# A fused attention and two MoE layers: a new order of the work, another load of the normalisation's gains, and a split last store

## The chip, the cores and the metric

The kernel runs on one core of a Trainium2 chip. The metric is the device time of one execution in microseconds, the median of three runs. A profile of one further execution goes with it; its times are those of that execution.

## The reference

The input has 4 batches of 576 tokens and 8 heads of 64. Three layers follow each other.

```
scores = q k^T / 8;  masked to 0 <= i - j < 64;  softmax;  x = attn v          # [2304, 512]
h  = x w_in;  s = h * softmax(h);  ln = (s - mean) / sqrt(var + 1e-6) * g_ln    # d_ff 1024
x2 = ln w_out                                                                   # [2304, 512]
h  = x2 w2_in;  g = (a0 + a1 h + a2 h^2 + a3 h^3) / (1 + |b0||h| + |b1| h^2 + 1e-6)   # d_ff 2048
out = g w2_out                                                                  # [2304, 512] float32
```

The MoE weights arrive as 64-bit floats.

## The kernel before

**Tiles and stages.** The 2304 tokens are 18 tiles of 128. Attention and the first MoE layer work tile by tile: `scores` (matmuls in PSUM, with the band mask added by matmuls with `ib` and `masks` for tiles 0 to 7, and by VectorE from `limits` for tiles 8 to 17), `max`, eight `exp` on ScalarE, `sum` and `rcp`, two `norm` on GpSimd, `probs` (transposes on TensorE), `probs_copy`, `attend`, `att_hi` and `att_lo` (x as a sum of two parts), `h0` to `h3` (one step for each 128 rows of w_in), then the softmax and normalisation of h, its transposes `lnT`, and for three tiles together `x2`. x2 goes to DRAM. The second MoE layer works on blocks of 4, 4, 4, 3 and 3 tiles: pairs of `g` steps, an elementwise chain on ScalarE and VectorE, and `o` steps. Each product is made of three matmuls with split operands, but for `h` of tiles 0 and 1, which use plain float32.

**Weights.** 64-bit words are turned into float32 by a chain of ScalarE and VectorE steps (`cv0` to `cv7`). The units are `i` (w_in: two halves of a half megabyte for rows 0 to 127, then three of one megabyte), `o` (w_out, four of one megabyte) and `c` (both weights of the second layer, sixteen of one megabyte). The `c` units are spilled to DRAM as float32 (`w2d`) and read back later. Two loaded units (`x64`) and two converted ones (`cA`) fit at a time.

**gT.** `g_ln` is loaded as [128, 8], column c holding elements 128c to 128c + 127, and multiplied by -0.5 on GpSimd (lines 842 and 843). The conversion of w_out's parts multiplies by it.

**The order.** Nothing is issued in the order of the code. Each piece of work is a *step* with an engine, a duration, needs and buffers; `Schedule` (line 29) works out an order in Python while the kernel is built. `latest` gives each step a due time, worked back from wanted times and from what needs it; the table `SHIFT`, one number for each group of steps, moves these due times. `arrange` then simulates: among the steps that can start at the earliest moment it picks the one with the earliest due time. A DMA's result counts as landed 2.0 us after the DMA's own duration (line 158), the DMA queue is one resource that starts at 0.9 us (`AT`), and `PORT` names VectorE steps that may not run beside GpSimd's. `RINGS` holds the number of buffers; q and k have two each, the scores one. `gaps` puts filler matmuls ahead of TensorE's early steps where the plan has idle time. The order that comes out is issued as it is: every engine, and the SP queue with all DMAs, runs its own list in order and waits where something is not ready. So the durations in the code are the planner's costs, not measured times, and they only decide the order.

**The end.** The last block's last tile is finished last: `o_last`, then `o_copy` (512 columns on ScalarE or VectorE) and `o_store` (256 KB from SP).

Of the kernel before, what the change touches and what calls it, by code (L numbers as in the profile page):

```python
# [28 lines left out]
class Schedule:  # L29
# [14 lines left out]
    PORT = ("cv1", "cv2", "cv3", "cv6", "cv7", "ln_apply", "w2")  # L44
    AT = {"DMA": 0.9, "POOL": 0.7, "DVE": 0.8, "ACT": 0.8}
# [54 lines left out]
    def arrange(self):  # L100
# [38 lines left out]
        while ready:  # L139
# [18 lines left out]
            done[key] = t + dur + (2.0 if e == "DMA" else 0.0), e  # L158
# [16 lines left out]
    def gaps(self):  # L175

        idle, end = {}, 0.0
        for t, _, key, e in self.order:
            if e == "PE":
                if key[0] == "h0":  # L180
                    break
                idle[key] = max(0, int((t - end - 0.3) / 0.25)) if end else 0
                end = t + self.steps[key][1][0]
        return idle
# [69 lines left out]
    "solu_max.s": -23.79, "solu_exp.s": -2.77, "solu_mul.s": 187.84, "ln_square.s": 171.01, "ln_eps.s": 70.47,  # L254
    "ln_var.s": -132.84, "ln_root.s": -12.34, "ln_newton.s": -33.03, "ln_apply.s": 195.97, "lnT0.s2": -32.79,
# [51 lines left out]


PLAIN = 8


NORMP = 0

# [6 lines left out]
def attention_moe_moe2(ctx: ExitStack, tc, q, k, v, w1, w1o, g_ln, w2, w2o, num, den, out):  # L320
# [5 lines left out]
    nc = tc.nc  # L326
# [850 lines left out]
```

## Time and profile before

| | us |
|---|---|
| median of three runs (710.07 to 711.42) | 710.61 |
| the profiled execution | 714.31 |
| its span, first to last instruction | 712.5 |
| TensorE busy | 686.9 (96%) |
| VectorE busy | 579.7 (81%) |
| ScalarE busy | 484.4 (68%) |
| GpSimd busy | 62.3 (9%) |

The profile's span covers the instructions; the execution's own time is 1.8 us longer. PE is TensorE, DVE is VectorE, ACT is ScalarE, POOL is GpSimd, SP is the engine that issues the DMAs; PEld is the loading of weights into TensorE. Busy shares are means over stages with different limits. Lines are those of the kernel before.

### The profile page before, as it was taken

How to read it: one execution, taken by the hardware profiler on the slowest of the kernel's cores; microseconds unless marked ns; L12 is line 12 of the kernel's file. 1: busy time of each engine (PE TensorE's matmuls, PEld its weight loads, DVE VectorE, ACT ScalarE, POOL GpSimd, SP SyncE). 2: the span in 40 equal slices, each digit the busy share in tenths (PEclk: the TensorE clock that was granted, in tenths of full speed). 3: DMA queues.
4: the chain of work that ended last, by engine and by line, in shares of the span. 5: the costliest groups of instructions: out<-in, count | busy, mean ns of one | idle time of the engine just before them, and what ended most of it. 6: DMA issues, size and time to landing. Idle time of an engine off the chain costs nothing.

```text
span 712.5 us, 11368 instructions
## 1 busy us (share of the span) xinstructions
PE 686.9 (96%) x4356; PEld 591.6 (83%) x4356; DVE 579.7 (81%) x863; ACT 484.4 (68%) x878; POOL 62.3 (9%) x96
## 2 busy tenths in 40 slices
PE   5799999999899999999999999999999999999997
PEld 5557789789788989998888888888888889999896
DVE  5799998889798854687999787888778877878773
ACT  5799976676676844667876566675755756566662
POOL 3333202112220120000000000000000000000000
PEclk9999999999999999999999999999999999999999
DMA  8966437775968414604331030000300001000101
GB/s 267 333 199 202 167 140 254 247 246 184 333 197 293 153 46 126 199 1 163 103 99 51 0 104 0 1 1 0 104 1 0 1 1 59 1 1 7 38 1 45
DMA packets 44982, 77.81 MB, mean 109 GB/s; under 512 B 4672, under 2 KB 23104, under 8 KB 44544
## 3 DMA queue, kind: packets, MB, share of 16 engines
q1 hardware_dynamic: 44928, 77.09, 32.6%
q8 instruction: 34, 0.56, 0.3%
q14 instruction: 20, 0.16, 0.1%
HBM read 59.25 MB, written 17.83 MB: 108 GB/s over the span
## 4 chain that ended last, share of the span: by engine, by line
PE 70%; DVE 12%; DMA 7%; ACT 7%; issue 2%; SPq 1%; ACTq 0%; DVEq 0%
PE hp L964 9%; PE hp L963 9%; PE hp L962 9%; PE o L1029 9%; PE o L1030 9%; PE o L1028 9%; DMA w2d<-cc 5%; PE x L747 3%; PE x L749 3%; PE x L748 3%; DMA xi<-in_moe_w_in_dram 1%; ACT P L501 1%; PE h L671 1%; PE h L670 1%; PE h L669 1%
## 5 line engine op out<-in xcount | busy, mean ns | idle before, releaser
L962 PE MATMUL hp<-x2h,w 128*128 128x512 f32 (+1 forms) x320 | 118.1, 369 | 0.0
L964 PE MATMUL hp<-x2h,w 128*128 128x512 f32 (+1 forms) x320 | 117.9, 368 | 0.0
L963 PE MATMUL hp<-x2l,w 128*128 128x512 f32 (+1 forms) x320 | 117.7, 368 | 0.0
L1030 PE MATMUL o<-w,gl 128*128 128x512 f32 x288 | 112.6, 391 | 0.0
L1029 PE MATMUL o<-w,gh 128*128 128x512 f32 x288 | 112.5, 391 | 0.0
L1028 PE MATMUL o<-w,gh 128*128 128x512 f32 x288 | 112.0, 389 | 0.0
L982 DVE SCALAR_TENSOR_TENSOR w<-r,b,w 128x1024 f32<-128x1024 f32 (+1 forms) x40 | 47.0, 1176 | 53.1 <-ACT r L976 53.1
L974 ACT ACTIVATE w<-hp,ab 128x1024 f32<-128x1024 f32 (+1 forms) x40 | 41.3, 1032 | 67.9 <-PE hp L964 47.7
L1013 ACT CAST gh<-t 128x1024 fp32r<-128x1024 f32 (+1 forms) x40 | 38.6, 965 | 58.1 <-PE o L1029 43.8
L747 PE MATMUL x<-lh,wo 128*128 128x384 f32 x192 | 66.0, 344 | 1.4 <-ACT xs L361 1.4
L962 PEld LDWEIGHTS hp<-x2h,w 128*128 128x128 f32 x320 | 60.1, 188 | 8.7
L963 PEld LDWEIGHTS hp<-x2l,w 128*128 128x128 f32 x320 | 60.1, 188 | 8.6
L964 PEld LDWEIGHTS hp<-x2h,w 128*128 128x128 f32 x320 | 60.1, 188 | 7.5
L749 PE MATMUL x<-lh,wo 128*128 128x384 f32 x192 | 64.3, 335 | 0.0
L748 PE MATMUL x<-ll,wo 128*128 128x384 f32 x192 | 64.3, 335 | 0.0
L1030 PEld LDWEIGHTS o<-w,gl 128*128 128x128 f32 x288 | 54.0, 188 | 11.2
L1029 PEld LDWEIGHTS o<-w,gh 128*128 128x128 f32 x288 | 54.1, 188 | 10.7
L1028 PEld LDWEIGHTS o<-w,gh 128*128 128x128 f32 x288 | 54.1, 188 | 10.5
L521 POOL TENSOR_TENSOR P<-P,rc 128x512 f32<-128x512 f32 x36 | 45.5, 1280 | 111.9 <-DVE rc L513 76.3
L669 PE MATMUL h<-wi,xh 128*128 128x512 f32 x128 | 50.7, 396 | 1.8 <-DVE st L686 1.7
L357 DVE TENSOR_TENSOR gl<-t,gh 128x1024 fp32r<-128x1024 f32 (+1 forms) x40 | 44.5, 1112 | 8.9 <-ACT gh L1013 8.9
L671 PE MATMUL h<-wi,xl 128*128 128x512 f32 x128 | 50.4, 394 | 0.3 <-DVE xl L357 0.2
(113 smaller groups left out, 1442.6 us busy)
## 6 DMA issues: line engine op xcount, KB each, us to landing
v<-in_v_dram SPq DMA_DIRECT2D x35, 256.0 KB, 4.6
xc<-in_moe_w_in_dram SPq DMA_DIRECT2D x16, 512.0 KB, 4.0
xc<-in_moe_w_out_dram SPq DMA_DIRECT2D x16, 512.0 KB, 5.7
w2d<-cc SPq DMA_DIRECT2D x16, 512.0 KB, 6.5
r<-w2d SPq DMA_DIRECT2D x32, 256.0 KB, 2.9
k<-in_k_dram SPq DMA_DIRECT2D x17, 384.0 KB, 4.9
q<-in_q_dram SPq DMA_DIRECT2D x18, 256.0 KB, 5.3
x2d<-xs SPq DMA_DIRECT2D x6, 768.0 KB, 6.4
```

Of the source, the lines that this page charges most:

```text
L669: nc.tensor.matmul(o, xh[:, c, :], wh, start=(c == 0), stop=False)
L671: nc.tensor.matmul(o, xl[:, c, :], wh, start=False, stop=(c == KC - 1))
L747: nc.tensor.matmul(o, wh, lh[:, f, :], start=(f == 0), stop=False)
L748: nc.tensor.matmul(o, wh, ll[:, f, :], start=False, stop=False)
L749: nc.tensor.matmul(o, wl, lh[:, f, :], start=False, stop=(f == FC1 - 1))
L962: nc.tensor.matmul(h, wh[:, sl], xh[:, c], start=(c == 0), stop=False)
L963: nc.tensor.matmul(h, wh[:, sl], xl[:, c], start=False, stop=False)
L964: nc.tensor.matmul(h, wl[:, sl], xh[:, c], start=False, stop=(c == KC - 1))
L982: nc.vector.scalar_tensor_tensor(out=w, in0=r, scalar=b1, in1=w, op0=ALU.mult, op1=ALU.add)
L1028: nc.tensor.matmul(o, gh[:, n, sl], wh, start=(f == 0), stop=False)
L1029: nc.tensor.matmul(o, gh[:, n, sl], wl, start=False, stop=False)
L1030: nc.tensor.matmul(o, gl[:, n, sl], wh, start=False, stop=(f == FC2 - 1))
```

## The change

The steps' work is nearly the same. What changes:

- All of `SHIFT` is new, and some of the planner's costs are, so that the order of every engine is another one.
- A DMA counts as landed after 2.3 us instead of 2.0 us, and the DMA queue starts at 1.5 us.
- `g_ln` is loaded as 8 rows of 128 elements into a cleared [128, 128] tile, transposed on TensorE into PSUM, and multiplied by -0.5 on VectorE from there. `h0` of tile 0 comes after it, since both use the same PSUM tile.
- `ident`, `gR` and `ib` are made first on GpSimd, then the masks; the limits are a step of their own behind.
- Five filler matmuls precede TensorE's first step.
- The last tile's copy is made in two halves of 256 columns on ScalarE and VectorE, each with a store of its own, one issued from ScalarE and one from SP.
- A branch that was never taken (`NORMP = 0`) is removed.

```diff
-    PORT = ("cv1", "cv2", "cv3", "cv6", "cv7", "ln_apply", "w2")
-    AT = {"DMA": 0.9, "POOL": 0.7, "DVE": 0.8, "ACT": 0.8}
+    PORT = ("cv1", "cv2", "cv3", "cv6", "cv7", "ln_apply", "w2", "max_scale", "sum")
+    AT = {"DMA": 1.5, "POOL": 0.7, "DVE": 0.8, "ACT": 0.8}
...
-            done[key] = t + dur + (2.0 if e == "DMA" else 0.0), e
+            done[key] = t + dur + (2.3 if e == "DMA" else 0.0), e
...
-                idle[key] = max(0, int((t - end - 0.3) / 0.25)) if end else 0
+                idle[key] = max(0, int((t - end - 0.3) / 0.25)) if end else 5
...
 SHIFT = {
-    "cv.i_0_0": -234.63, "cv.i_0_512": 71.67, "cv.i_2_0": 195.23, "cv.i_3_0": 193, "cv.o_0": 120.63,
-    "load_q.1": -26.18, "load_k.1": 5.41, "load_v0.0": 95.7, "load_v1.0": 1.71, "load_q.2": 0.09, "load_k.3": -3.15,
...
+    "cv.i_0_0": -434.33, "cv.i_0_512": 87.02, "cv.i_1_0": 1.81, "cv.i_2_0": 203.88, "cv.i_3_0": 204.67, "cv.o_0": 122.97,
+    "load_k.1": -0.8, "load_v0.0": 17.18, "load_v1.0": 16.34, "load_q.2": 68.07, "load_q.3": -11.97, "load_k.3": 42.51,
...
     def constants():
+        make_identity(nc, ident)
+        nc.gpsimd.memset(gR, 0.0)
+        nc.gpsimd.tensor_copy(ib, ident)
         nc.gpsimd.memset(band, 0.0)
...
+    def make_limits():
...
-        make_identity(nc, ident)
-        nc.gpsimd.tensor_copy(ib, ident)
...
+    def gT_rows():
+        nc.tensor.transpose(h_tile(0)[:, 0:P], gR, ident)
+
+    def gT_scale():
+        nc.vector.tensor_scalar_mul(gT, tiles["h", 0][:, 0:FC1], -0.5)
...
+            needs += [("gT", 0)] if (t, c) == (0, 0) else []
...
-    add(("constants", 0), "POOL", 4.5, None, [], constants)
-    add(("gT_load", 0), "DMA", 0.1, -60.0, [], lambda: nc.sync.dma_start(gT, g_ln.rearrange("(c p) -> p c", p=P)))
-    add(("gT", 0), "POOL", 0.3, None, [("gT_load", 0)], lambda: nc.gpsimd.tensor_scalar_mul(gT, gT, -0.5))
+    add(("constants", 0), "POOL", 3.9, None, [], constants)
+    add(("limits", 0), "POOL", 2.2, None, [("constants", 0)], make_limits)
+    add(("gT_load", 0), "DMA", 0.1, -60.0, [("constants", 0)], lambda: nc.sync.dma_start(gR[0:FC1], g_ln.rearrange("(c p) -> c p", p=P)))
+    add(("gT_rows", 0), "PE", 0.2, None, [("gT_load", 0)], gT_rows)
+    add(("gT", 0), "DVE", 0.12, None, [("gT_rows", 0)], gT_scale)
...
-            add(("cvl", *key), "DMA", 2.7, None, [], cv_load, key, *load, take=[("x64", key)], group=group)
+            add(("cvl", *key), "DMA", 2.55 if key[0] == "o" else 3.3, None, [], cv_load, key, *load, take=[("x64", key)], group=group)
...
-            add(("cv7", *key), "DMA", 1.46, want, [("cv6", *key)], cv_spill, key, give=[("cA", key)], group=group)
+            add(("cv7", *key), "DMA", 1.8, want, [("cv6", *key)], cv_spill, key, give=[("cA", key)], group=group)
...
-        add(("cvl", *key), "DMA", 1.42 if key[1] == 0 else 2.7, None, [], w1_load, key[1], cols,
+        add(("cvl", *key), "DMA", 1.35 if key[1] == 0 else 2.55, None, [], w1_load, key[1], cols,
...
+    def o_half(bk, j, n):
...
+        o = tiles["o", bk][j][:, n * DM // 2:(n + 1) * DM // 2]
+        copy((nc.scalar, nc.vector)[n], tiles["os", bk, j][n], o)
+
+    def o_store_half(bk, j, n):
+        r0 = (FIRSTS[bk] + j) * P
+        (nc.scalar, nc.sync)[n].dma_start(out[r0:r0 + P, n * DM // 2:(n + 1) * DM // 2], tiles["os", bk, j][n])
```

`SHIFT` has some 530 entries before and after; the lines of it shown here are put together from entries that concern the first loads.

## Rows read from the trace of the kernel before

**Rows 1.** The page's head.
```profile
span 712.5 us, 11368 instructions
```
**Rows 2.** Busy time by stage: PE, PEld, DVE, ACT, POOL; clock; DMA share; GB/s.
```profile
0.00:30.00 30.00, 19.28 (x220) 16.68 (x221) 19.10 (x29) 18.34 (x48) 11.39 (x28) 0.94 0.84 297
30.00:100.00 70.00, 65.08 (x673) 49.44 (x673) 68.53 (x131) 68.41 (x197) 17.72 (x25) 1.00 0.59 199
100.00:250.00 150.00, 143.76 (x1207) 128.59 (x1206) 131.81 (x319) 106.69 (x269) 27.65 (x34) 1.00 0.69 230
250.00:709.00 459.00, 458.75 (x2261) 396.90 (x2259) 360.29 (x387) 290.63 (x367) 5.51 (x10) 1.00 0.14 44
709.00:712.50 3.50, 0.00 (x0) 0.00 (x0) 0.00 (x0) 0.37 (x1) 0.00 (x0) 0.75 0.36 137
```
**Rows 3.** Timeline, 15 to 32 us: start, duration, work, idle time before and its releaser.
```profile
16.08 0.20 DVE L513 RECIPROCAL rc<-rc 128x8 f32<-128x8 f32 x1
...
17.84 0.26 POOL L843 TENSOR_SCALAR gT<-gT 128x8 f32<-128x8 f32 x1 [10.86 <-DMA gT<-in_moe_g_ln_dram]
18.07 3.09 POOL L521 TENSOR_TENSOR P<-P,rc 128x512 f32<-128x512 f32 x2
...
21.94 1.12 ACT L599 ACTIVATE xi<-xi 128x1024 f32<-128x1024 f32 x1 [4.03 <-DMA xi<-in_moe_w_in_dram]
...
23.09 0.69 DVE L604 TENSOR_SCALAR xi<-xi 128x1024 f32<-128x1024 f32 x1 [1.65 <-ACT xi L599]
...
24.00 0.59 ACT L361 COPY PT<-pt 128x512 f32<-128x512 f32 x1
...
26.38 0.17 DVE L509 TENSOR_SCALAR rc<-sum 128x8 f32<-128x8 f32 x1 [1.39 <-ACT P L504]
...
28.44 3.70 PE L663 MATMUL h<-xi,xh 128*128 128x512 f32 x8 [0.76 <-ACT xh L361]
```
**Rows 4.** Timeline of the SP queue, same columns.
```profile
3.13 7.12 SPq L450 DMA_DIRECT2D k<-in_k_dram  x2
...
12.06 0.58 SPq L581 DMA_DIRECT2D xi<-in_moe_w_in_dram  x1
...
14.69 2.89 SPq L443 DMA_DIRECT2D q<-in_q_dram  x2
```
**Rows 5.** DMA issues of the whole span: KB each, median us to landing.
```profile
w2d<-cc SPq DMA_DIRECT2D x16, 512.0 KB, 6.5
...
xi<-in_moe_w_in_dram SPq DMA_DIRECT2D x3, 1024.0 KB, 9.9
...
gT<-in_moe_g_ln_dram SPq DMA_DIRECT2D x1, 4.0 KB, 6.3
```
**Rows 6.** Two slices of the stage table; the last two columns are the DMA's.
```profile
14.00:15.00 1.00, 1.00 (x11) 1.00 (x10) 0.86 (x2) 1.00 (x5) 0.00 (x0) 1.00 0.63 137
...
16.00:17.00 1.00, 1.00 (x36) 0.94 (x35) 0.68 (x3) 1.00 (x2) 0.00 (x0) 1.00 1.00 410
```
**Rows 7.** Waits of ACT and PE, 100 to 250 us: total, times, longest.
```profile
ACT cc L599 <- DMA w2d<-cc: 19.7, 9, 5.3
...
PE pv L547 <- ACT PT L361: 3.7, 3, 1.6
```
**Rows 8.** Groups by shape (busy us, mean ns), and landings of the output's 18 stores.
```profile
L361 ACT COPY xs<-x 128x384 f32<-128x384 f32 x22 | 10.4, 473 | 13.4 <-PE x L749 10.8 <-DMA x2d<-xs 2.5
L361 ACT COPY os<-o 128x512 f32<-128x512 f32 x18 | 9.4, 592 | 6.0 <-PE o L1030 6.0
...
L363 DVE COPY xs<-x 128x384 f32<-128x384 f32 x2 | 1.1, 551 | 0.0
...
DMA to landing us min/median/max: 2.0/2.4/4.4
```
**Rows 9.** Timeline of PE: scores of tile 0 and of tile 1.
```profile
7.84 1.99 PE L478 MATMUL s<-k,q 64*64 64x128 f32 x32 [0.15 <-DMA q<-in_q_dram]
...
16.14 1.04 PE L478 MATMUL s<-k,q 64*64 64x128 f32 x32
```

More of the change, by code (lines that the diff above doesn't have):

```diff
@@ L208 @@
 SHIFT = {
[45 rows of a table removed]
-    "solu_max.s": -23.79, "solu_exp.s": -2.77, "solu_mul.s": 187.84, "ln_square.s": 171.01, "ln_eps.s": 70.47,
-    "ln_var.s": -132.84, "ln_root.s": -12.34, "ln_newton.s": -33.03, "ln_apply.s": 195.97, "lnT0.s2": -32.79,
[30 rows of a table removed]
-    "cv.c_15": -82.41, "load_coefficients.s": -15.43, "coefficients.s": 8.16, "close_attention.s": 11.01,
[16 rows of a table removed]
-    "g_hi.s": -21.03, "g_lo.s": 33.55, "o.s": -2.06,
[41 rows of a table added]
+    "h2.s2": -16.25, "h3.s2": 6.13, "solu_max.s": -11.77, "solu_mul.s": 3.5, "ln_square.s": 13.76, "ln_eps.s": -5.59,
+    "ln_var.s": -0.88, "ln_root.s": -1.46, "ln_apply.s": 71.68, "lnT0.s2": 57.07, "ln_hi0.s": 1.13,
[46 rows of a table added]
+    "g_n1.s": 32.93, "g_n2.s": 31.85, "g_hi.s": -12.04, "g_lo.s": 5.83, "o.s": 45.65,
 }
@@ L309 @@
 PLAIN = 8
-NORMP = 0
 RINGS = {"q": 2, "k": 2, "v": 4, "s": 1, "P": 2, "tr": 2, "PT": 4, "o": 2, "x": 2, "h": 1, "e": 2, "lnT": 2, "xs": 1,
@@ L384, in attention_moe_moe2 @@
     ident = cst.tile([P, P], F32, name="ident")
+    gR = cst.tile([P, P], F32, name="gR")
     ib = ap.tile([P, P], BF16, name="ib", tag="ib", bufs=1)
@@ L387, in attention_moe_moe2 @@
     limits = ap.tile([P, 3, P], F32, name="limits", tag="limits", bufs=1)
+    band = ap.tile([P, WIN], F32, name="band", tag="band", bufs=1)
     def constants():
-        band = ap.tile([P, WIN], F32, name="band", tag="band", bufs=1)
+        make_identity(nc, ident)
+        nc.gpsimd.memset(gR, 0.0)
+        nc.gpsimd.tensor_copy(ib, ident)
         nc.gpsimd.memset(band, 0.0)
@@ L503, in soft_exp @@
             return
-        nc.scalar.activation((tiles["s", t] if t < NORMP else Pn[t])[:, j, n, :], tiles["s", t][:, j, n, :], AF.Exp,
-                             bias=mx[:, c:c + 1], scale=0.125, accum_out=su[:, c:c + 1])
+        nc.scalar.activation(Pn[t][:, j, n, :], tiles["s", t][:, j, n, :], AF.Exp, bias=mx[:, c:c + 1], scale=0.125,
+                             accum_out=su[:, c:c + 1])
     def soft_sum(t):
@@ L513, in soft_rcp @@
         nc.vector.reciprocal(rc, rc)
-    def soft_norm_all(t):
-        nc.vector.tensor_tensor(out=Pn[t].rearrange("p j c k -> p (j c) k"), in0=tiles["s", t].rearrange("p j c k -> p (j c) k"),
-                                in1=stat[t][2].unsqueeze(2).broadcast_to([P, H, P]), op=ALU.mult)
     def soft_norm(t, j):
@@ L789, in attention_moe_moe2 @@
                 if t >= PLAIN:
-                    step(f"max{j}{n}", "DVE", 0.24, ["scores", ("constants", 0)], soft_max_of, t, j, n, give=[("s", t)])
-                step(f"exp{j}{n}", "ACT", 0.342, ["max_scale" if t < PLAIN else f"max{j}{n}"], soft_exp, t, j, n,
-                     give=[("s", t)] if NORMP <= t < PLAIN else [])
+                    step(f"max{j}{n}", "DVE", 0.215, ["scores", ("limits", 0)], soft_max_of, t, j, n, give=[("s", t)])
+                step(f"exp{j}{n}", "ACT", 0.342 if t < PLAIN else 0.392, ["max_scale" if t < PLAIN else f"max{j}{n}"], soft_exp, t, j, n,
+                     give=[("s", t)] if t < PLAIN else [])
         step("sum", "DVE", 0.12, [f"exp{j}{n}" for j in range(2) for n in range(4)], soft_sum, t)
         step("rcp", "DVE", 0.12, ["sum"], soft_rcp, t)
-        if t < NORMP:
-            step("norm", "DVE", 1.14, ["rcp"], soft_norm_all, t, give=[("s", t)])
-        for j in range(2) if t >= NORMP else ():
+        for j in range(2):
             step(f"norm{j}", "POOL", 1.08, ["rcp"], soft_norm, t, j)
         for j in range(2):
-            step(f"probs{j}", "PE", 0.44, [f"norm{j}" if t >= NORMP else "norm"], probs_T, t, j, want=WANT[f"probs{j}"], take=[("tr", (t, j))],
+            step(f"probs{j}", "PE", 0.44, [f"norm{j}"], probs_T, t, j, want=WANT[f"probs{j}"], take=[("tr", (t, j))],
                  give=[("P", t)])
@@ L838, in attention_moe_moe2 @@
                      take=[] if dc else [("xs", pr)], give=[("o", (t, 2 + dc))])
-            step("x2_store", "DMA", 1.5, ["x2_out3"], x2_store, pr, give=[("xs", pr)])
-    add(("constants", 0), "POOL", 4.5, None, [], constants)
-    add(("gT_load", 0), "DMA", 0.1, -60.0, [], lambda: nc.sync.dma_start(gT, g_ln.rearrange("(c p) -> p c", p=P)))
-    add(("gT", 0), "POOL", 0.3, None, [("gT_load", 0)], lambda: nc.gpsimd.tensor_scalar_mul(gT, gT, -0.5))
+            step("x2_store", "DMA", 2.2, ["x2_out3"], x2_store, pr, give=[("xs", pr)])
+    add(("constants", 0), "POOL", 3.9, None, [], constants)
[3 more added lines that the diff above has]
+    add(("gT", 0), "DVE", 0.12, None, [("gT_rows", 0)], gT_scale)
     def convert(key, want, *load):
@@ L1044, in o_store @@
         nc.sync.dma_start(out[r0:r0 + P, :], tiles["os", bk, j])
+    def o_half(bk, j, n):
+        if n == 0:
+            tiles["os", bk, j] = [pools["tp"].tile([P, DM // 2], F32, name=f"os{bk}_{j}_{m}", tag="xr", bufs=RINGS["xr"])
+                                  for m in range(2)]
+        o = tiles["o", bk][j][:, n * DM // 2:(n + 1) * DM // 2]
[3 more added lines that the diff above has]
+        (nc.scalar, nc.sync)[n].dma_start(out[r0:r0 + P, n * DM // 2:(n + 1) * DM // 2], tiles["os", bk, j][n])
     G = {3: 2.09, 4: 2.73}
@@ L1128, in attention_moe_moe2 @@
             for j in range(SIZES[bk]):
+                if (bk, j) == (NB2 - 1, SIZES[bk] - 1):
+                    for n, (e, d) in enumerate((("ACT", 0.3), ("DVE", 0.33))):
+                        add((f"oc{n}", bk, j), e, d, s3 + 2.0 + 0.1 * j, [("ol", j)], o_half, bk, j, n,
+                            take=() if n else [("xr", ("o", bk, j))])
+                        add((f"os{n}", bk, j), ("ACT", "DMA")[n], 0.4, s3 + 2.6 + 0.1 * j, [(f"oc{n}", bk, j)], o_store_half, bk, j, n)
+                    continue
                 add(("oc", bk, j), "ACT|DVE", (0.475, 0.6), s3 + 2.0 + 0.1 * j, [("ol", j) if bk == NB2 - 1 else ("o", i)], o_copy, bk, j,
```

178 rows, old and new, of the table SHIFT are left out of this document.

## The prediction

> **What bounds the kernel now.** I read the page first: the span is 712.5 us [rows 1]. Then the table by stages [rows 2]: from 250 us to 709 TensorE is busy in 458.75 of 459 us, so whatever is gained or lost before 250 us reaches the end one for one, and nothing behind 250 us but the tail can be gained by an order. TensorE's idle time sits in the first 30 us (10.7 us, and part of what is counted busy there is filler matmuls without use), in 30 to 100 us (4.9), in 100 to 250 us (6.2) and in the tail (3.5). The same table names the limits: in 30 to 100 us VectorE is busy in 68.53 of 70 us and ScalarE in 68.41, so that stage lasts as long as their work does, and it ends earlier only if that work starts earlier. In 100 to 250 us VectorE is at 88%, ScalarE at 71%: waits decide there, not the sum of work.
>
> Last the timeline of the start [rows 3]. The first h matmul of tile 0 begins at 28.44. Behind it lie two waits in program order. GpSimd's normalisation of tile 0 had its reciprocal at 16.28 (16.08 + 0.20) but began at 18.07, because the scaling of gT stood ahead of it in GpSimd's queue and waited for its DMA until 17.84. ScalarE sat idle for 4.03 us until 21.94, waiting for the third megabyte of w_in; the exponentials of tile 1 and the copy of tile 0's transposed probabilities (24.00) stood behind that instruction. VectorE lost 1.65 and 1.39 us in its wake.
>
> **The start: gT as rows, constants first.** *Removed from GpSimd:* one instruction of 0.26 us and its wait; the normalisation of tile 0 can begin 18.07 - 16.28 = 1.8 us sooner. Next late is then ScalarE's wait for w_in, which ends at 21.94 in either case, so alone this gains little at 28.44.
>
> *The load.* The column load of gT is 1,024 elements for 4 KB, with 6.3 us to landing [rows 5]. While it is in flight, the DMA engines move 137 GB/s at a share of 0.63 in one microsecond, against 410 at 1.00 in a later one [rows 6]: 0.63 x 410 - 137 = 121 KB, 0.3 us of full rate lost in that slice. As eight rows that goes; I count it as part of the gain on w_in's landing.
>
> *Added:* clearing gR on GpSimd (the clearing of ident's like size is some 0.2 us, an estimate by the 0.26 of gT's own instruction, rows 3), one transpose on TensorE and one small VectorE multiply. VectorE is full in the stage that follows, so the multiply counts: between 0 and the 0.26 us of the same operation on GpSimd; I take +0.2. The transpose costs nothing while TensorE waits anyway between scores 0, which ends at 9.83, and scores 1, which begins at 16.14 [rows 9]. It waits for a load that SP can issue once gR is clear, about where it issued its sixth load (3.13, rows 4); with the same 6.3 us it lands near 10. In TensorE's queue scores 1 and the probabilities of tile 0 stand behind it. The cover is some 6 us, and each microsecond beyond that is one microsecond later.
>
> *Constants.* The identity and the masks come first, the limits in a step behind. The first real scores matmul, at 7.84, waits for no constant but for q and k, so the time there is 0; the limits are read only from tile 8 on. The bound on the loss side is 0 too, since the same instructions run in the same queue, all done before the normalisation at 16 us. Five fillers now precede TensorE's first step. Scores 0 took 1.99 us where scores 1 took 1.04 [rows 9]; whether fillers that end some microseconds earlier change that, no row shows: between 0 and -0.95, and I take 0, as the matmuls right ahead of scores 0 did not help it either.
>
> The Trainium skill (TensorE: Matmul & The Clock Gate, "What's actually happening") has the array throttled by default and released by activity. Rows 9 agree in the durations, a factor of 1.9. By that rule the fillers could make scores 0 run at 2.4 GHz, and the sum would be 0.95 us lower; I let it widen the low end only.
>
> **The order, computed anew.** I can't list the new order, but some of it follows from the planner's rule, the earliest due among what can start, with the costs in the diff. (They tell the order, not a time.) In the plan before, the first full megabyte of w_in behind the opening loads starts after 0.9 + 1.42 + 0.66 + 1.0 + 1.0 + 0.66 + 2.7 + 1.0 + 1.42 + 0.66 + 0.1 = 11.5 and has landed at 11.5 + 2.7 + 2.0 = 16.2; the trace has 21.94. In the new plan, the shifts put both halves of v, the next q and tile 1's v ahead of it: 1.5 + 1.35 + 0.66 + 1.0 + 1.0 + 0.66 + 2.55 + 0.1 + 1.0 + 1.32 + 0.66 + 1.35 + 1.32 = 14.5, landed at 14.5 + 2.55 + 2.3 = 19.3. So ScalarE's waiting instruction moves back by 3.1 us in the plan, behind the exponentials of tile 1 and the copy. These fit into the 4.03 us of idle time. On VectorE, which sets the next 70 us, the gain is at most its two waits, 1.65 + 1.39 = 3.0 us. The loss is bounded by the slower case below, 5.1. I take half of the gain, **-1.5**: the megabyte still lands about where it did, and its conversion can't start sooner.
>
> In 100 to 250 us the costliest wait is ScalarE's for the spills of converted weights: 19.7 us in 9 waits, 5.3 the longest [rows 7]. Behind it TensorE waits for ScalarE's copies, 3.7 us, the largest part of its 6.2 us. The planner's spill took 1.46 + 2.0 = 3.46 us, now 1.8 + 2.3 = 4.1; the trace has 6.5 [rows 5]. That closes 0.64 of 3.04 us, a fifth, and a fifth of 6.2 us is 1.3. Between -6.2 (all idle time gone) and +5.3 (one more wait as the longest, in full on TensorE) I take **-1.0**, near that fifth.
>
> **The tail.** ScalarE's copy of 512 columns takes 0.59 us, of 384 columns 0.47 [rows 8], so one of 256 is about 0.35; VectorE's of 384 takes 0.55, and one of 256 between two thirds of that, 0.37, and 0.55. They run side by side: 0.59 - 0.42 = 0.17 saved. The store itself: the 18 stores of this kind took 2.0 to 4.4 us to landing [rows 8]. Two halves carry the same bytes, one of them by ScalarE's queue, of which no row shows a use; I bound the store's change by -1.0 (half of the shortest) and +2.4 (from the shortest to the longest), and take 0, as the bytes are the same: sum **-0.2**. TensorE's last matmul does not move.
>
> The Trainium skill (DMA: Bandwidth & Descriptors, "Rules for kernel authors") speaks against the two queues: transfers issued from SP and ScalarE run on the same 16 engines and interleave, and only issue time is saved. By it the tail gains the copy's part alone; by the most that the bounds allow the sum would be 1.0 us lower.
>
> **Sum.** -1.5 - 1.0 - 0.2 + 0.2 = -2.5 us. The profiled execution took 714.31 us by the clock of the device (span 712.5 and 1.8 around it), so it would be 711.8. The median of the runs shown is 710.61, 3.7 below that execution; the same difference gives **708.1**.
>
> **Rivals.**
> *Hidden (710.3).* The planner's landings are still short: 2.55 + 2.3 = 4.85 us for a megabyte that took 9.9, 4.1 for a spill that took 6.5 [rows 5]. So the in-order waits stay, some elsewhere, and the start gains nothing, since VectorE's work is the same. Left are -0.2 and +0.2 and some -0.3 by the lighter gT load. For it: the wait for w_in ends by bytes, not by order. Against: 3.1 us of shift in the plan against 4.03 of idle time.
>
> *Both stages pay fully (704).* VectorE's 3.0 us and half of the 6.2 us of idle time: -3.0 - 3.1 - 0.4 = -6.5. For it: the idle time is there. Against: the spill's cost is corrected by a fifth only.
>
> *Slower (712.2): SP stands still ahead of w_in.* SP issues in order, and a load whose buffer is not free holds up all behind it: the two k loads at 3.13 took until 10.25 [rows 4], since k has two buffers and the third k waited for scores 0, and the two q loads at 14.69 took until 17.58, until scores 1 had freed a buffer. In the new plan w_in's last two megabytes start at 14.5, and by then scores 1 is planned as done. If q and k of tile 3 get in ahead, SP holds w_in until scores 1 really ends at 17.18 [rows 9] instead of issuing it at 12.06 [rows 4]. That is 5.1 us later. If the transfer takes as long as it did, all of it comes out; if it has the engines to itself, 1,049 KB at 410 GB/s [rows 6] and the 2.0 us of the shortest store land it at 21.8, and nothing does. The middle is +2.6 us for ScalarE and VectorE; less the 1.0 us of the middle stage, +1.6. It decides from the point where these two stand ahead of w_in in SP's queue. For it: the planner thinks scores 1 done sooner than it is. Against: it needs both loads ahead of both megabytes.
>
> **How the numbers follow.** Forecast 0.45 (own range 706.0 to 709.2), hidden 0.25, both stages 0.13, slower 0.17. Some 0.2% (1.4 us) is what a measurement here can tell from no change: faster 0.57 (0.13 and 0.44 of the 0.45), same 0.26 (0.25 and the rest of it), slower 0.17. The range runs from the large gain, 704.0, to the slower case's 712.2; beyond it I leave half of each, some 0.06 below and 0.09 above.
>
> **What would show it.** On GpSimd no instruction waits for gT, and the normalisation of tile 0 begins near 16.3. ScalarE's exponentials of tile 1 come before its wait for the third megabyte. The first h matmul begins near 26. TensorE's idle time in 100 to 250 us falls to some 5 us, ScalarE's waits for spills below 19.7. After TensorE's end some 3.5 us remain. Wrong would be: SP holding w_in for scores 1; the transpose of gT waiting on TensorE past 16 us; or a start that gains while the middle gives it back by new waits for spills.

## The result, and the profile after

| | us | ratio to before |
|---|---|---|
| before, median of 4 runs (710.07 to 711.42) | 710.85 | |
| after, median of 4 runs (703.60 to 704.39) | 704.16 | 0.9905 [0.9888, 0.9923] |

The change saves 6.7 us where 2.5 were forecast. The direction was right. The time lies in the range, at its low end, and outside the forecast's own range of 706.0 to 709.2. The profiled execution of after took 703.60 us.

The first profile of before is a poor partner for a comparison: its execution took 714.31 us, 3.5 above the median. So the same kernel was profiled once more (`before_again`, 711.61 us), and after is set against that one. Page heads, after and then before_again:

```profile
span 701.8 us, 11398 instructions
PE 687.4 (98%) x4369; PEld 593.6 (85%) x4369; DVE 578.9 (82%) x862; ACT 483.5 (69%) x881; POOL 61.1 (9%) x96
```
```profile
span 709.8 us, 11368 instructions
PE 686.2 (97%) x4356; PEld 590.7 (83%) x4356; DVE 578.7 (82%) x863; ACT 484.5 (68%) x878; POOL 61.3 (9%) x96
```

Busy time by stage, after, with the columns of [rows 2] (the stage of 100 to 250 us is split at 130):

```profile
0.00:30.00 30.00, 23.11 (x236) 19.26 (x237) 19.48 (x33) 20.49 (x56) 9.74 (x28) 0.94 0.87 302
30.00:100.00 70.00, 66.10 (x706) 50.55 (x706) 68.26 (x148) 68.76 (x205) 19.40 (x26) 1.00 0.62 206
100.00:130.00 30.00, 30.00 (x216) 27.09 (x215) 25.52 (x42) 17.96 (x34) 5.10 (x6) 1.00 0.48 154
130.00:250.00 120.00, 120.00 (x1062) 108.78 (x1062) 107.34 (x268) 90.58 (x233) 23.29 (x28) 1.00 0.70 243
250.00:696.00 446.00, 446.00 (x2147) 386.40 (x2146) 357.93 (x373) 284.68 (x356) 3.52 (x8) 1.00 0.14 44
```
The same of before_again:
```profile
0.00:30.00 30.00, 20.96 (x228) 16.90 (x229) 19.99 (x33) 20.49 (x57) 10.60 (x28) 1.00 0.90 317
30.00:100.00 70.00, 65.06 (x679) 50.51 (x678) 68.53 (x131) 68.77 (x191) 17.58 (x24) 1.00 0.56 191
100.00:130.00 30.00, 29.79 (x206) 25.84 (x205) 28.07 (x62) 19.00 (x45) 6.99 (x8) 1.00 0.71 222
130.00:250.00 120.00, 114.33 (x1003) 102.96 (x1002) 102.56 (x255) 85.90 (x221) 22.50 (x29) 1.00 0.67 231
```
The filler matmuls alone, in the first 30 us, of after and then of before_again; they count as busy and do no work:
```profile
0.00:30.00 30.00, 12.05 (x80) 11.02 (x80) 0.94 0.87 302
```
```profile
0.00:30.00 30.00, 9.91 (x68) 9.36 (x68) 1.00 0.90 317
```

Read as a ledger of TensorE, whose end sets the end: in the first 30 us it does 23.11 - 12.05 = 11.06 us of real work after and 20.96 - 9.91 = 11.05 before, so the start gives **0**. (Some of the 11.06 is the same work at a lower granted clock: attend of tile 0, the mask matmuls and scores 2 took 1.61 + 0.64 + 1.92 us in after and 1.19 + 0.41 + 1.10 in before_again; see the last section.) In 30 to 100 us it does 66.10 against 65.06, **-1.0**. That difference is the order's and not one execution's: the five profiles that follow the new order there have 65.93 to 66.13 us, the five that follow the old one 64.30 to 65.08. In 100 to 250 us it idles 0.00 us after and 0.21 + 5.67 = 5.88 before, **-5.9**. Behind that it never idles in either, as forecast. The tail gives -0.1 (below), and TensorE's busy time without the fillers came out 0.9 us shorter in all (687.4 - 12.05 = 675.4 against 686.2 - 9.91 = 676.3). Together that is the 8.0 us between the two spans. The medians lie 6.7 apart: these two executions were 0.6 below and 0.8 above theirs, so the terms carry about that much uncertainty together.

**The middle.** ScalarE's largest wait in 100 to 250 us and its wait for spills, after (total, times, longest); [rows 7] has the latter before, 19.7 us in 9 waits:

```profile
ACT PT L353 <- PE pt L521: 19.5, 9, 4.2
...
ACT cc L600 <- DMA w2d<-cc: 5.0, 4, 2.7
```
The waits for spills (`w2d`) are down to a quarter, and ScalarE now waits for TensorE, as an engine off the path should. TensorE has no waits in that stage at all; [rows 7] had it waiting for ScalarE's copies. One of the old waits in place, before_again:

```profile
126.20 0.33 SPq L573 DMA_DIRECT2D xc<-in_moe_w_in_dram  x1
126.57 0.43 SPq L573 DMA_DIRECT2D xc<-in_moe_w_out_dram  x1
127.05 0.43 SPq L641 DMA_DIRECT2D w2d<-cc  x1
...
133.56 1.15 ACT L599 ACTIVATE cc<-xc 128x1024 f32<-128x1024 f32 x1 [5.24 <-DMA w2d<-cc]
134.95 1.10 ACT L361 COPY PT<-pt 128x512 f32<-128x512 f32 x2
136.10 1.15 PE L547 MATMUL pv<-PT,v 128*64 128x64 f32 x32 [1.19 <-ACT PT L361]
```
ScalarE's next conversion needs the buffer that the spill empties. The spill was issued right behind a megabyte that shares the DMA engines, ScalarE stood still for 5.24 us in program order, tile 9's copies stood behind it, and TensorE waited for them.

**The start.** Timeline of after, to be read against [rows 3] and [rows 9]:

```profile
6.89 1.98 PE L476 MATMUL s<-k,q 64*64 64x128 f32 x32 [1.93 <-DVE xi L607]
...
15.89 2.04 POOL L515 TENSOR_TENSOR P<-P,rc 128x512 f32<-128x512 f32 x2 [8.84 <-DVE rc L511]
...
19.36 1.18 ACT L600 ACTIVATE xi<-xi 128x1024 f32<-128x1024 f32 x1 [0.35 <-DMA xi<-in_moe_w_in_dram]
...
23.30 1.61 PE L541 MATMUL pv<-PT,v 128*64 128x64 f32 x32 [2.52 <-ACT PT L353]
...
25.26 1.92 PE L476 MATMUL s<-k,q 64*64 64x128 f32 x32
...
27.11 3.72 PE L664 MATMUL h<-xi,xh 128*128 128x512 f32 x8
```
The same places in before_again:
```profile
17.04 0.26 POOL L843 TENSOR_SCALAR gT<-gT 128x8 f32<-128x8 f32 x1 [9.95 <-DVE xi L604]
17.27 2.04 POOL L521 TENSOR_TENSOR P<-P,rc 128x512 f32<-128x512 f32 x2
...
19.57 1.18 ACT L599 ACTIVATE xi<-xi 128x1024 f32<-128x1024 f32 x1 [1.55 <-DMA xi<-in_moe_w_in_dram]
...
26.13 3.70 PE L663 MATMUL h<-xi,xh 128*128 128x512 f32 x8 [0.43 <-ACT xh L361]
```
The megabyte whose landing [rows 3] showed at 21.94 was there at 19.57 in this execution of the same kernel, and the first h matmul began at 26.13, not 28.44. After has GpSimd's normalisation 1.4 us sooner than before_again: its reciprocal ended 0.7 us sooner (15.71 against 16.38), and the rest is the wait for gT. Its first h matmul is 1.0 us later, but that again belongs to executions. The first h matmul begins at 25.7 to 27.0 us in the six profiles besides the first that start in the old order, and at 25.7 to 27.1 in the five that start in the new one.

**The tail.** After, timeline of the last work:

```profile
697.80 0.39 PE L1032 MATMUL o<-w,gl 128*128 128x512 f32 x1
698.23 0.37 ACT L353 COPY os<-o 128x256 f32<-128x256 f32 x1 [0.77 <-PE o L1032]
698.63 0.37 ACTq L1058 DMA_DIRECT2D out_dram<-os  x1
698.63 0.42 DVE L355 COPY os<-o 128x256 f32<-128x256 f32 x1 [6.56 <-ACT os L353]
```
The DMA issues of the two halves, KB each and us to landing:
```profile
out_dram<-os ACTq DMA_DIRECT2D x1, 128.0 KB, 1.8
out_dram<-os SPq DMA_DIRECT2D x1, 128.0 KB, 1.7
```
The copies don't run side by side: VectorE's half begins when ScalarE's has ended. From TensorE's end (697.80 + 0.39) to the end of the span are 3.61 us, against 3.75 in before_again (705.66 + 0.39 to 709.8). All eleven profiles with two halves have 3.59 to 3.67 us there, the three with one store 3.75 to 3.80.

### The profile page after: what moved, and what is told of

Same layout as the page of the kernel before. It is cut to its first block, busy times and chain, and to the rows that moved or that the text cites. A ratio compares the mean times of both kernels' runs of the same rounds, so it can differ in the third digit from the quotient of the medians.

```text
span 701.8 us, 11398 instructions
## 1 busy us (share of the span) xinstructions
PE 687.4 (98%) x4369; PEld 593.6 (85%) x4369; DVE 578.9 (82%) x862; ACT 483.5 (69%) x881; POOL 61.1 (9%) x96
## 4 chain that ended last, share of the span: by engine, by line
PE 88%; DVE 6%; ACT 3%; DMA 2%; issue 1%; SPq 0%
PE hp L966 9%; PE hp L965 9%; PE o L1031 9%; PE hp L964 9%; PE o L1032 9%; PE o L1030 9%; PE x L748 5%; PE x L750 5%; PE x L749 5%; PE h L670 3%; PE h L672 3%; PE h L671 3%; PE s L476 2%; DMA xi<-in_moe_w_in_dram 2%; PE pv L541 2%; PE pl L730 2%
## 5 line engine op out<-in xcount | busy, mean ns | idle before, releaser
L670 PE MATMUL h<-wi,xh 128*128 128x512 f32 x128 | 50.9, 397 | 2.2 <-DVE st L687 2.2
L671 PE MATMUL h<-wi,xh 128*128 128x512 f32 x128 | 50.0, 391 | 0.0
```

Of the source, the lines that this page charges most:

```text
L670: nc.tensor.matmul(o, xh[:, c, :], wh, start=(c == 0), stop=False)
L671: nc.tensor.matmul(o, xh[:, c, :], wl, start=False, stop=False)
```

## The experiments

All but the first and the last two replace the planner by a list: `FIXED` names every step with its engine in the order of a known plan, and nothing is planned.

```diff
 def arrange(self):
-    ...
+    self.order = [(0.0, i, k, e) for i, (k, e) in enumerate(FIXED)]
+    self.idle = dict(IDLE)
```

### The kernel before, once more

No edit.

> The kernel before once more, for a second profile: the first profiled execution took 714.31 us, 3.5 us over the median of 710.85. If those 3.5 us were a peculiarity of that execution, this one has a span near 709 and TensorE idle for less than 6.2 us between 100 and 250 us, perhaps 3 to 4. If they belong to the kernel, the span is near 712 again and the idle time near 6.

Measured: 711.61 us, span 709.8. TensorE's idle time in 100 to 250 us is 5.9 us, as in the first profile (6.2), while the first h matmul begins 2.3 us sooner. So the middle's idle time belongs to the kernel, and the late start belonged to one execution.

### The load as rows, in the old order

```diff
 # FIXED is the old order, with:
+ ("limits") behind ("constants");  ("gT_rows","PE"), ("gT","DVE") behind ("scores",1)
+ two halves of the last copy and store in place of one
- ("gT","POOL")
```

> The order before, written out and kept, with only the new load of gT, the constants' new order and the two halves at the end. Theory A (the new order makes the gain, most of it in 100 to 250 us): 710 to 711, no more than 1 us gained. Theory B (the removed wait of GpSimd and the lighter load carry the start, and the start carries the end): 707 to 709, and the first h matmul is near 27.

Measured: 711.28 against 711.08, ratio 1.0002 [0.9992, 1.0012], ten runs of it. Timeline of this kernel:

```profile
17.42 0.17 DVE L561 TENSOR_SCALAR gT<-h 128x8 f32<-128x8 f32 x1 [1.91 <-PE h L558]
...
18.08 2.04 POOL L515 TENSOR_TENSOR P<-P,rc 128x512 f32<-128x512 f32 x2 [10.96 <-DVE rc L511]
```
Where it was put, behind scores 1, the wait moved from GpSimd to VectorE and the normalisation was no sooner. That is partly the place's doing, so the opposite test was made too.

### The new order with the old load

```diff
-gT_load: nc.sync.dma_start(gR[0:FC1], g_ln.rearrange("(c p) -> c p", p=P))
+gT_load: nc.sync.dma_start(gT, g_ln.rearrange("(c p) -> p c", p=P))
-gT_rows on PE, gT on DVE
+gT on POOL: nc.gpsimd.tensor_scalar_mul(gT, gT, -0.5)
```

> The new order, kept, with gT loaded as a column and scaled on GpSimd as before. If the load is worth nothing, as it was in the old order: 703.5 to 705. If the removed wait of GpSimd and the lighter load are worth what the start's timeline suggests in an order that uses them: 705.5 to 707.

Measured: 702.91 against 710.88, ratio 0.9887 [0.9853, 0.9922]. That is below both expected ranges; the gain is all there without the load as rows. In neither order is the load worth anything that can be measured.

### Where in the order the gain lies

Joins of the two orders: up to a point one list, then all that is left in the sequence of the other. The sixteen `c` units are renumbered so that both convert them in the same sequence.

```diff
-FIXED = new order
+FIXED = steps of one order up to 91, 95 or 131 us of its plan, then the rest as the other has it
```

> The new order for all steps planned before 95 us, then the order before for the rest. Theory A: the start gives 2 to 3 us of the 6.7, the old order behind it keeps its waits for spills: 707.5 to 709, TensorE idle 4 to 6 us in 100 to 250 us. Theory B (the start decides): 704 to 705.5.

> The order before for all steps planned before 95 us, then the new order. Theory A: the middle gives 4 us or so: 706 to 707.5, TensorE idle under 1.5 us in 100 to 250 us. Theory B: 709 to 711. If start and middle add up, the gains of this run and of the one before it sum to about 6.7 us.

> The join at 95 us left 39 steps on one side only, 12 us of VectorE, ScalarE and TensorE work that the other order had counted on; its run waited 3.2 us for VectorE right behind the join. This join is at the point where the two orders have done nearly the same: 11 steps differ. Old order until 91 us of the plan, then the new one. Theory A (the order behind the start makes the gain): 704 to 706.5, no TensorE idle time in 125 to 250 us. Theory B (start and rest only gain together): 709 to 711.

> Old order until 131 us of the plan, then the new one; again 11 steps differ at the join. If the gain lies behind 131 us, where 4.5 us of TensorE's 5.9 us of idle time lie in the second profile of before, 705 to 707. If it lies in 91 to 131 us (where tile 6's h is put ahead of the first x2), 709 to 711. The loss against the run with the join at 91 is what that stretch is worth.

> The complement: new order until 131 us, then the old. With the gain behind 131 us: 709 to 711, ScalarE's waits for spills near 18 us and TensorE idle for 4 us or more in 130 to 250 us. With the gain before it: 705 to 707.

| kernel | ratio to before | us |
|---|---|---|
| new to 95, old behind | 1.0010 [0.9994, 1.0027] | 712.09 |
| old to 95, new behind | 0.9983 [0.9974, 0.9992] | 709.70 |
| old to 91, new behind | 0.9946 [0.9931, 0.9961] | 707.89 |
| old to 131, new behind | 0.9923 [0.9907, 0.9939] | 706.51 |
| new to 131, old behind | 1.0057 [1.0040, 1.0073] | 715.83 |

Of the five times the fourth lies in the range of the theory that the gain is behind the join, the second in that of the other theory, and the rest in neither. The gains of the first two, -1.0 and 1.4 us against their own median of before (711.08), sum to 0.4 and not to 6.7. Windows of the fourth and then of the fifth:

```profile
130.00:250.00 120.00, 119.16 (x1059) 108.00 (x1057) 103.69 (x252) 87.68 (x224) 24.92 (x29) 1.00 0.67 228
```
```profile
130.00:250.00 120.00, 112.00 (x949) 100.91 (x948) 101.95 (x254) 86.10 (x219) 20.28 (x26) 0.97 0.69 240
```
The new rest behind 131 us (this kernel has the load and the tail of after too) brings 711.74 - 706.51 = 5.2 us, and TensorE's idle time there falls from 5.67 us to 0.84. The old rest keeps idle time there: 5.41 us behind the join at 95. Behind the join at 131 it is 8.00 us, but one wait of 5.0 us, for VectorE at 144.26, is the join's own. That leaves 3.0 us, and ScalarE's waits for spills came to 10.1 us where near 18 were expected, so this run shows less than it was made for. The join at 95 with the new rest has a wait of its own too, of 3.19 us at 112.04. So the first two rows of the table and the fifth, as a split of the gain, say little; the third and fourth bound from below what the new rest brings, if a join can only cost time. What the new first 131 us add (0.9905 against 0.9923) is not clear of the noise in the times, as the intervals overlap; the ledger has 1.0 us for it, in 30 to 100 us.

### The spill ahead of the megabyte

In SP's queue of before, 7 spills stand directly behind the load of a later unit. They change places; all else stays. Then the same for 8 spills in after.

```diff
 # FIXED, each such pair:
-("cvl","c",m) ... ("cv7","c",n)
+("cv7","c",n) ... ("cvl","c",m)
```

> The order before, kept, but for 7 spills: each is put ahead of the megabyte of weights that SP issued right ahead of it. Nothing else moves. Theory A1 (ScalarE's waits for spills hold TensorE): a spill lands about 2 us sooner, ScalarE's 19.7 us of waits for them fall to 12 or less, TensorE's idle time falls by 2 to 3 us and the time to 708 to 709.5. Theory A2 (the waits for spills are mostly slack, the place of ScalarE's and VectorE's instructions holds TensorE): the waits fall, the time stays within 710 to 711.5.

> The new order, kept, but for 8 spills that are put ahead of the megabyte of weights issued right ahead of them. Theory A1 (spills cost only where TensorE waits in their wake): the new order has no TensorE idle time in 100 to 250 us, so nothing can be gained: 703.5 to 705. Theory A3 (loads and spills cost time as such, by the engines they keep busy): 701 to 703.

Measured, before: 708.55 against 711.74, ratio 0.9959 [0.9947, 0.9971], so 0.0041 x 711.74 = 2.9 us less. After: 703.71, ratio to before 0.9901 [0.9869, 0.9934], against 0.9905 unswapped: nothing. The swapped kernel of before, timeline of the place shown above:

```profile
125.34 0.33 SPq L641 DMA_DIRECT2D w2d<-cc  x1
125.76 1.12 SPq L573 DMA_DIRECT2D xc<-in_moe_w_in_dram  x1
...
132.43 1.16 ACT L599 ACTIVATE cc<-xc 128x1024 f32<-128x1024 f32 x1 [5.61 <-DMA xc<-in_moe_w_out_dram]
...
134.99 1.15 PE L547 MATMUL pv<-PT,v 128*64 128x64 f32 x32 [0.22 <-ACT PT L361]
```
Its window of 130 to 250 us:
```profile
130.00:250.00 120.00, 117.10 (x1016) 105.21 (x1015) 101.01 (x255) 85.85 (x221) 22.26 (x28) 1.00 0.65 227
```
Its waits of ScalarE in 100 to 250 us:
```profile
ACT cc L599 <- DMA xc<-in_moe_w_out_dram: 11.0, 5, 5.6
ACT cc L599 <- DMA w2d<-cc: 7.6, 4, 2.8
```
A spill now lands 4.1 us after its issue in the median, against 6.6 in before_again. TensorE's idle time in 130 to 250 us falls from 5.67 to 2.90 us: half of it came from spills behind loads. ScalarE waits hardly less in all, 11.0 + 7.6 = 18.6 us against 19.7, for now the megabyte lands last; but the conversion starts 1.1 us sooner (132.43 against 133.56), and TensorE's wait behind it shrinks from 1.19 to 0.22. In after, ScalarE's waits for spills fall from 5.0 to 1.0 us, and TensorE, which had no idle time to lose, gains nothing. A wait that TensorE does not follow was worth nothing here.

### Due times and costs apart

```diff
 # one kernel: the new SHIFT, with the old planner's costs
-PORT with "max_scale", "sum"; AT 1.5; landing 2.3; loads 2.55 and 1.35; spill 1.8
+PORT without; AT 0.9; landing 2.0; loads 2.7 and 1.42; spill 1.46; ...
 # the other: the old SHIFT, with the new costs
```

> The kernel after with the new table SHIFT, but the planner's costs of before (landing 2.0, spill 1.46, loads 2.7 and 1.42, start 0.9, PORT without max_scale and sum). Theory S (the searched due times make the order): 703.5 to 706. Theory L (the measured landings make it): 707 to 711, with ScalarE's waits for spills back above 12 us in 100 to 250 us.

> The kernel after with the old table SHIFT and the new costs of the planner. Theory L: 705 to 709. Theory S: the old due times were found against the old costs, so 710 to 720. If both crosses lose, the due times and the costs only work together.

Measured: 729.06 (ratio 1.0264 [1.0226, 1.0303]) and 725.73 (1.0208 [1.0177, 1.0238]). Both lose in 30 to 100 us, where TensorE had 66.10 us of work after; the windows of the two, in this order:

```profile
30.00:100.00 70.00, 60.02 (x591) 45.01 (x590) 60.56 (x114) 60.66 (x175) 16.12 (x20) 0.88 0.55 182
```
```profile
30.00:100.00 70.00, 59.98 (x542) 44.55 (x543) 63.76 (x106) 56.83 (x147) 15.14 (x20) 0.90 0.48 158
```
Neither half of the planner's change is the gain, nor a share of it. These due times fit only the costs that they were made with; what runs is the order that the two give together.

## Why the prediction was right, and where it was wrong

**Behind 250 us: right.** TensorE is never idle there in either kernel, so what is won ahead of it reaches the end.

**The start, -1.5: measured 0, and -1.0 from 30 to 100 us.** The step that failed is the use of one execution's timeline as the kernel's. ScalarE's 4.03 us and VectorE's 1.65 and 1.39 us [rows 3], from which half was taken, were 1.55 us for ScalarE in the second profile and 1.15 us for VectorE, in one wait. The bound of the start was worked out from a delay that mostly was not there, so "Hidden" was right about the first 30 us. The -1.0 behind them is real, but no run shows which waits it comes from. The plan worked out by hand failed too: SP had issued the first full megabyte behind the opening loads by 11.47 us in after (10.42 + 1.05) and issued it at 12.16 in before_again, so it came sooner and not 3.1 us later. Two of the marks put up for it failed: the exponentials of tile 1 still stand behind ScalarE's wait for the third megabyte (a wait of 0.35 us now), and the first h matmul began at 27.11, not near 26. One came true: no GpSimd instruction waits for gT, and the normalisation begins at 15.89. The transpose of gT ran at 11.97, between fillers. Both lead to nothing, since attend of tile 0 begins only at 23.30, behind ScalarE's second copy of the transposed probabilities: in after ScalarE makes both copies, at 21.13 and 22.63, among the exponentials, where before_again has one on VectorE at 21.64. This place in the new order the prediction could not see. The term of some -0.3 for the lighter load, counted in it, was 0 in both orders, as far as the times can tell. The multiply on VectorE, +0.2 in the sum, took 0.16 us.

**The middle, -1.0: measured -5.9.** This is the term that was mis-sized, and it makes up for the rest and more. The working took the share by which the planner's cost of a spill came nearer to the measured landing, a fifth, and applied it to the idle time. The runs show that the one does not set the other. The spills take 6.2 us to landing after (6.5 before, [rows 5]) and the new plan still reckons with 4.1, yet TensorE's idle time is gone; and with the new costs but the old due times the kernel is 2% slower. The mechanism itself, spill, ScalarE in order, copies, TensorE, was named rightly, and the swap of spill and load confirms it for half of the idle time (2.8 of 5.67 us). The end that should have been taken seriously was the bound of -6.2: the idle time was scattered over waits that an order can avoid, on a stage where VectorE and ScalarE were not full.

**The tail, -0.2: measured -0.14.** The prices of the halves were right (0.35 and 0.42 expected, 0.37 and 0.42 measured); "side by side" was wrong. In series they take 0.37 + 0.03 + 0.42 = 0.82 us, longer than the 0.59 of one copy [rows 8], but the first half's store is issued before the second is copied, and each half lands in 1.8 and 1.7 us, where the shortest of the whole stores took 2.0.

**The fillers ahead of scores 0, taken as 0: nothing in after, but not always.** Scores 0 took 1.98 us there with five fillers ahead and 1.99 without [rows 9], and 1.98 or 1.99 in five more profiles with the same fillers. In the seventh, new_order_old_load, it took 1.10:
```profile
6.86 1.10 PE L476 MATMUL s<-k,q 64*64 64x128 f32 x32 [1.91 <-DVE xi L607]
```
The granted clock reads 1.00 over scores 0 in this profile and in after alike, so the difference shows in the durations alone, and what decides it was not tested. The rule from the Trainium skill (TensorE: Matmul & The Clock Gate, "What's actually happening") that activity releases the throttle, by which the fillers could have been worth 0.95 us, is borne out by this one profile and not by the six others.

**The slower case did not come.** Half of its condition did: q of tile 3 stands ahead of w_in's last loads. But as the third q loaded, into two buffers, it had to wait for scores 0, which ended at 8.87, and not for scores 1; before, SP had waited until 10.25 [rows 4]. SP's queue in after, timeline: q of tile 3, the last three loads of w_in, and behind them k of tile 4, which came after scores 1 and held up nothing of w_in.
```profile
8.92 0.35 SPq L441 DMA_DIRECT2D q<-in_q_dram  x1
...
10.42 1.05 SPq L582 DMA_DIRECT2D xi<-in_moe_w_in_dram  x2
...
11.99 0.44 SPq L582 DMA_DIRECT2D xi<-in_moe_w_in_dram  x1
17.09 0.38 SPq L448 DMA_DIRECT2D k<-in_k_dram  x1
```

**"Both stages"** named the number that was measured, 704, but not its parts: the start paid nothing in the first 30 us and 1.0 behind them, and the middle all of its idle time instead of half. That the range reached down to 704.0 is owed to this rival, which had a chance of 0.13; that its sum met the time is luck. (The 0.4 us in that sum is not worked out; tail, multiply and load give 0.3.)

**Still open.** By which single moves the new order avoids the second half of the waits behind 131 us: spills stand behind loads in it as often as before (8 and 7 times), and ScalarE comes to its conversions at other points of TensorE's work, but no run isolates one such move. A third buffer for converted weights, which might take the wait away, was not tried. No version that was run is clearly faster than after: the intervals of the new order with the old load, 0.9887 [0.9853, 0.9922], and of after, 0.9905 [0.9888, 0.9923], overlap almost wholly.

## What to carry to other kernels

Take a second profile before pricing anything in the first 30 us of a kernel; what two executions of the same kernel disagree on is not the kernel's. In the stage where VectorE and ScalarE were not full, TensorE's whole idle time was within reach of an order, so keep that end of the range likely in such a stage. Where an engine waits in order for a small transfer, try issuing it ahead of the bulk load that nobody waits for yet: here that gave 2.9 us where TensorE waited in its wake, and nothing where it did not. Due times held only for the costs that they were found with: change both together or neither.

## What the runs showed of the hardware

The granted clock fell in after when TensorE had waited 2.52 us for ScalarE's copy, to 23.30. One slice of its stage table behind that:

```profile
24.00:25.00 1.00, 1.00 (x22) 0.88 (x22) 0.64 (x2) 1.00 (x3) 0.00 (x0) 0.50 1.03 404
```
At 0.50, which is 1.2 GHz, scores 2 took 1.92 us. In new_order_old_load TensorE waited longer at the same place, 2.91 us, and the clock stayed at 1.00, so the length of the wait alone does not decide:
```profile
23.41 1.15 PE L541 MATMUL pv<-PT,v 128*64 128x64 f32 x32 [2.91 <-ACT PT L353]
...
24.74 1.10 PE L476 MATMUL s<-k,q 64*64 64x128 f32 x32
```
From the beginning of attend of tile 0 to the first h matmul are 3.81 us in after (23.30 to 27.11) and 2.57 in new_order_old_load (23.41 to 25.98): the lower clock cost some 1.2 us there. Whether that reaches the end is not shown. before_again, at a clock of 1.00, took 3.80 us for the same (22.33 to 26.13), because TensorE waited for ScalarE in it, 0.56 us ahead of the mask matmuls and 0.43 ahead of h.

Two engines that read two halves of one PSUM tile ran one behind the other (0.37 and then 0.42 us). By the profile VectorE's wait ended with ScalarE's copy; whether the hardware or the program makes it wait there was not tested.
